# Sliding-window attention and an MLP on one core: more blocks' q and k transposed by DMA, and v's loads asked for first

## The chip, the cores and the metric

The kernel runs on one core of a Trainium2 chip. The metric is the device time of one execution in microseconds. The kernel before took a median of 314.43 us over three runs (312.98, 314.43 and 316.19). The profiled execution is a fourth one and took 316.07 us.

## The reference

Eight batches of eight heads attend over 576 tokens with 64 elements per head, in a causal window of 128 tokens with a linear distance bias per head. The result, laid out as 512 elements per token, is normalised without a bias, goes through an MLP with a hidden width of 2048, and is added to the MLP's output.

```python
scores = scale * np.matmul(q, k.transpose(0, 1, 3, 2))
mask = (rel >= 0) & (rel < window)                    # window = 128
scores = np.where(mask, scores + bias[None], -1000000000.0)
attn = np.exp(scores - np.max(scores, axis=-1, keepdims=True))
attn = attn / (np.sum(attn, axis=-1, keepdims=True) + 1e-09)
x = np.matmul(attn, v)                                # then (B, S, H * D)
xn = (x - mu) / np.sqrt(var + 1e-06) * g_ln
out = x + np.maximum(xn @ w_ch1, 0.0) @ w_ch2
```

## The kernel before

**Blocks and groups.** Two batches form a pair and a pair has nine blocks of 128 tokens, 36 blocks in all, numbered 0 to 35 in the list `order`. Within a pair, blocks 0 to 7 alternate between the two batches, and the ninth (`T = 8`) holds the last 64 tokens of both. An even block of a pair brings q and k for itself and its odd neighbour. So in the running numbers, q and k arrive with blocks 0, 2, 4, 6, 8, then 9, 11, 13, 15, 17, then 18, 20, 22, 24, 26, then 27 and so on; 8, 17, 26 and 35 are the tails. The MLP takes the blocks in groups: four groups of two blocks, then seven groups of four. Group 4 is blocks 8 to 11, group 5 is blocks 12 to 15.

**Loads.** The list `loads` (L247 to L256) holds, block by block, q and k (where the block is even in its pair) and then v, with the weights in between. `load_until` (L259) issues this list up to a place; the step of block n asks for everything up to block `n + AHEAD`, with one more block for n above 8 (L675). All these loads convert from float32 to float16 and are issued by POOL. The engines PE, DVE, ACT and SP run in the order in which the program emits their instructions. POOL is left to the compiler's own planner, which issues what it finds ready.

**Turning q and k.** The scores need q and k with the head's elements on the partitions. There are two ways. Up to block 17, `load_qk` (L198) loads two neighbouring tokens in one piece, so that a packet writes 256 bytes, with two DMAs for q and two for k. Then `turn` (L300) transposes 64x64 pieces on PE through `transposed` (L284): 64 transposes for a block (32 for a tail). DVE and ACT copy the result out of PSUM, with two copies each (one each for a tail). From block `TURN_BY_DMA = 18` on, `load_natural` (L211) loads single tokens (128 bytes a packet), with four DMAs for q and two for k. Then `turn_natural` (L321) issues DMA transposes on SP's queue: two for q and two for k (one each for a tail).

**Buffers.** The loaded q and k stand in `raw_pool`, four buffers each. A load waits until the block four earlier in the list of q and k has been turned. The turned q and k stand in `turned_pool`, four buffers each. v stands in ten buffers, so a load of v for block n waits for the last reader of block n - 10, which is `values_at_once` of block n - 8.

**The steps.** A hand-written list of steps is woven between the MLP's matmuls by `weave_at`. For n from 8 on, block n gives four steps (L674 to L692): the loads, the masks, `values_at_once` of n and `centre` of n with half of the scores of block n + 2; then the other half, with `turn` of block n + 3 where it is turned on PE; then masks, the square of n, and `turn_natural` of q for block n + 4 and of k for block n + 5 where these are turned by DMA; then masks again. `centre` (L512) makes `xc` on DVE and, from block 8 on, issues one DMA transpose on SP that writes the block's columns of the group's `xT`. `mlp1` of a group reads all of `xT`. SP also issues the output stores.

**The gain g.** `g_line` (one partition) and `g_row` (128 partitions) are constants, used by `spread_g`, by a copy in `turn_first`, and by `centre` of blocks 0 to 3 (L531). The output tiles `o` come from `out_pool`, with five buffers under one tag.

Of the kernel before, what the change touches and what calls it, by code (L numbers as in the profile page):

```python
# [10 lines left out]
FP16 = mybir.dt.float16  # L11
FP32 = mybir.dt.float32
# [5 lines left out]
P = 128  # L18
# [6 lines left out]
HALF = P // 2  # L25
GROUPS = [2] * 4 + [4] * 7

NV = 10
AHEAD = 6

FIRST_GROUPS, FIRST = 2, 4

# [3 lines left out]

SEVEN = 4

TURN_BY_DMA = 18


SUMS_AT = {
# [30 lines left out]
def kernel(  # L73
# [12 lines left out]
    DM = H * D  # L86
# [3 lines left out]
    HP = H // 2  # L90
# [4 lines left out]
    def pool(name, bufs, **kw):  # L95
        return ctx.enter_context(tc.tile_pool(name=name, bufs=bufs, **kw))

    consts = pool("consts", 1)
    raw_pool = pool("raw", 4)
    turned_pool = pool("turned", 4)  # L100
    probs_pool = pool("probs", 4)
    x_pool = pool("x", 14)
    xc_pool = pool("xc", 5)
# [2 lines left out]
    out_pool = pool("outp", 5)  # L106
# [30 lines left out]

    g_sb = consts.tile([P, NKB], FP32)
    nc.sync.dma_start(out=g_sb, in_=moe_g_ln.rearrange("(kb p) -> p kb", p=P))
    g_line = consts.tile([1, DM], FP32)  # L140
    nc.sync.dma_start(out=g_line, in_=moe_g_ln.rearrange("(o d) -> o d", o=1))
    g_row = consts.tile([P, DM], FP32)
    one_line = consts.tile([1, P], FP32)
    magic = consts.tile([P, 4], I32)
    ones = consts.tile([P, 4 * P], FP16)
# [87 lines left out]
    def by_dma(p, blk):  # L233
        return p * NSLOT + blk >= TURN_BY_DMA

# [9 lines left out]
    order = [(p, blk) for p in range(NPAIR) for blk in range(NSLOT)]  # L245
    w1s, w2s = ([(f, c) for c in range(4)] for f in (load_w1, load_w2))
    weights = {3: w1s + w2s[:2], 5: w2s[2:]}  # L247
    loads, place = [], []
    for n, (p, blk) in enumerate(order):
        if blk % 2 == 0:  # L250
            for src, tag in ((q, "q"), (k, "k")):
                load = load_natural if by_dma(p, blk) else load_qk
                loads.append((load, src, tag, p, blk // 2))
        loads.append((load_v, p, blk))
        place.append(len(loads))
        loads += weights.get(n, [])  # L256
    issued = 0
# [11 lines left out]
    turned = {}  # L269
# [30 lines left out]
    def turn(p, i, in_sc=False, copies=(nc.vector.tensor_copy, nc.scalar.copy)):  # L300

        ps = [bank(b if in_sc else None) for b in range(2)]
        k = keys_tile("k", p, i)
        if i < 4:
            q = queries(p, i)
            transposed("q", p, i, [t[:, 0] for t in ps])  # L310
            transposed("k", p, i, [t[:, 1] for t in ps])
            for b, copy in enumerate(copies):
                copy(out=q[:, b], in_=ps[b][:, 0])
                copy(out=k[:, b].rearrange("p h (c r) -> p r h c", r=2), in_=ps[b][:, 1])  # L314
        else:
            q = keys_tile("q", p, i)
            for tag, t, dst, copy in zip("qk", ps, (q, k), copies):
                transposed(tag, p, i, [t[:, 0]])
                copy(out=dst[:, 0].rearrange("p h (c r) -> p r h c", r=2), in_=t[:, 0])

    def turn_natural(tag, p, i):  # L321

        st = raw.pop((tag, p, i))
        t = turned_pool.tile([P, HP, 2, P], FP16, tag=tag, name=tag)
        turned[tag, p, i] = t.rearrange("p h b q -> p b h q")
        for b in range(2 if i < 4 else 1):
            nc.sync.dma_start_transpose(
                out=t[:, :, b], in_=st[:, b].rearrange("p h d -> p (h d)")
            )
# [6 lines left out]
        )  # L336

    def queries(p, i):
        t = turned_pool.tile([P, 2, 2, HP, HALF], FP16, tag="q", name="q")
        turned["q", p, i] = t.rearrange("p b r h c -> p b h r c")  # L340
        return t

    def keys_tile(tag, p, i):
        t = turned_pool.tile([P, 2, HP, P], FP16, tag=tag, name=tag)
        turned[tag, p, i] = t
        return t

    def turn_first():

        q, k = queries(0, 0), keys_tile("k", 0, 0)  # L350
        ps = [bank(b)[:, 0] for b in range(2)]
        transposed("q", 0, 0, ps)
        for b in range(2):
            nc.vector.tensor_copy(out=q[:, b], in_=ps[b])
        ps_row = spread_g()
        warm(2)
        ps = [bank(b)[:, 0] for b in (0, None)]
        transposed("k", 0, 0, ps)
        for b, copy in enumerate((nc.scalar.copy, nc.vector.tensor_copy)):
            copy(out=k[:, b].rearrange("p h (c r) -> p r h c", r=2), in_=ps[b])  # L360
        nc.vector.tensor_copy(out=g_row, in_=ps_row)
# [67 lines left out]
    def attends(p, blk):  # L429

        low, high, every = [0, 1], [2, 3], [0, 1, 2, 3]
        if blk == T:
            return [(p, T, [6, 7], m_ends, "probs", hps) for hps in (low, high)]
        if blk < 2:
            return [(p, blk, [blk], m_full[:, :, P:], "own", every)]
        return [(p, blk, [blk - 2, blk], m_full, "probs", hps) for hps in (low, high)]
# [5 lines left out]
    def tail_attend(p):  # L442
        return (p, T, [T], m_tail, "own", [0, 1, 2, 3])
# [166 lines left out]
    for g, size in enumerate(GROUPS):  # L610
        n = sum(GROUPS[:g])
# [3 lines left out]
    count = len(order)  # L615

    def turn_step(n, *how):
        p, blk = order[n]
        return [(turn, p, blk // 2) + how]

    def scores_step(n):
        return [(scores,) + order[n]]

    def values_steps(n):
        p, blk = order[n]
        ahead = place[min(n + AHEAD + (n > TURN_BY_DMA - 10), count - 1)]
        return [
            [(load_until, ahead), (masks, p, blk), (values, p, blk, 0)],
            [(values, p, blk, 1), (centre, p, blk)],
        ]  # L630

    def x_step(n, copy=nc.vector.tensor_copy):
        return [(turn_x,) + home[n] + order[n] + (copy,)] if n < BY_DMA else []

    def variance_of(n):

        return [(variance, n)] + [(inv_std, n - 3, 4)] * (n % 4 == 3)

    def masks_of(n, *halves):
        return [(masks,) + order[n] + halves]  # L640

    def warm_step(n):
        return [[(warm, n)]]


    steps = warm_step(11) + [[(turn_first,)]] + warm_step(3)
    steps += [scores_step(0), scores_step(1) + masks_of(0) + masks_of(1)] + warm_step(6)
    steps += values_steps(0)
    steps += [turn_step(2, True, (nc.scalar.copy, nc.scalar.copy))]
    steps += values_steps(1) + warm_step(4)  # L650
    steps += [x_step(0, nc.scalar.copy)] + warm_step(2) + [scores_step(2)]
    steps += [masks_of(2, 1) + x_step(1) + scores_step(3), values_steps(2)[0]]
    steps += [masks_of(2)]
    first = len(steps)
# [10 lines left out]
    steps += [values_steps(5)[0], turn_step(6, True), values_steps(5)[1], scores_step(6)]  # L665
    steps += [x_step(5) + masks_of(6), scores_step(7) + variance_of(4), values_steps(6)[0]]

    steps += [values_steps(6)[1], x_step(6) + masks_of(7), *values_steps(7)]
    steps += [x_step(7) + variance_of(5) + variance_of(6)]
    steps += [turn_step(8) + variance_of(7), scores_step(8) + turn_step(9)]  # L670
    steps += [[(scores_tail, 0)] + scores_step(9) + masks_of(8)]


    for n in range(8, count):  # L674
        ahead = place[min(n + AHEAD + (n > TURN_BY_DMA - 10), count - 1)]  # L675
        todo = []
        if n + 1 < count and order[n + 1][1] == T:
            todo.append(tail_attend(order[n][0]))
        if n + 2 < count:
            todo += attends(*order[n + 2])  # L680
        step = [(load_until, ahead), (masks,) + order[n]]
        step += [(values_at_once,) + order[n], (centre,) + order[n]]
        step += [(attend, *args, 1) for args in todo[:1]]
        second = [(attend, *args, 1) for args in todo[1:]]
        if n + 3 < count and order[n + 3][1] % 2 == 0 and not by_dma(*order[n + 3]):
            second += turn_step(n + 3)
        third = [(masks, *args[:2], 1) for args in todo[:1]] + [(square, n)]
        for tag, m in (("q", n + 4), ("k", n + 5)):
            if m < count and order[m][1] % 2 == 0 and by_dma(*order[m]):
                p, blk = order[m]  # L690
                third.append((turn_natural, tag, p, blk // 2))
        steps += [step, second, third, [(masks, *args[:2], 1) for args in todo[1:]]]  # L692
# [355 lines left out]
```

## Time and profile before

| | us |
|---|---|
| Median of three runs (lowest, highest) | 314.43 (312.98, 316.19) |
| The profiled execution | 316.07 |
| Its span, first to last instruction | 314.3 |
| Mean granted TensorE clock over the span | 0.994 |
| DVE busy, ACT busy, POOL busy | 233.9, 184.4, 107.9 |
| 64x64 transposes of q and k on PE (L294) | 576, of which 320 after 58 us |
| DMA transposes on SP: xT, k, q | 28, 18, 18 |
| Their time from issue to landing, median: xT, k, q | 4.4, 4.2, 5.5 |

A group of instructions has a line of the kernel, an engine, the tiles that it writes and reads, a count, its busy time and the mean of one. Idle time ahead of an instruction is put down to whatever released it last. The chain of waits follows the last instruction back to what it waited for; in its listing each row has a start, a length and a name. PE's instructions overlap, so the busy time of PE doesn't say how fast it works; the granted clock beside it does.

### The profile page before, as it was taken

What the parts mean: (1) busy time and instruction counts of PE and PEld (TensorE: products, weight loads), DVE (VectorE), ACT (ScalarE), POOL (GpSimd) and SP (SyncE); (2) the same over time, 40 slices, a digit from 0 to 9 for tenths busy, and PEclk for the clock granted to TensorE, in tenths of its full rate; (3) what the DMA queues carried; (4) which work ended last, traced back from release to release, by engine and by line L of the source; (5) the groups of instructions that cost most, each with busy time, mean ns of one, the idle gap of its engine ahead of it and who ended that gap; (6) DMA issues with size and microseconds to landing.
All of it is one profiled execution on the core that took longest, in us unless ns stands there. A gap on an engine that the chain in (4) does not pass through costs nothing.

```text
span 314.3 us, 9387 instructions
## 1 busy us (share of the span) xinstructions
PE 302.9 (96%) x3886; PEld 200.8 (64%) x3886; DVE 233.9 (74%) x629; ACT 184.4 (59%) x330; POOL 107.9 (34%) x148
## 2 busy tenths in 40 slices
PE   8889999998988999999999999999999999999994
PEld 3468655856733568755864686468656865785583
DVE  2689887697993889767976887688769876964563
ACT  6588766767944983467357735753676268405600
POOL 8923758769341634725251645120000000000000
PEclk9999999999997999999999999999999999999999
DMA  9999999999992999999999999993562143025004
GB/s 105 176 206 198 189 146 173 199 146 151 131 117 53 95 105 125 138 197 106 134 126 166 101 141 138 165 135 59 114 108 50 37 94 79 17 19 134 0 19 117
DMA packets 140316, 36.99 MB, mean 118 GB/s; under 512 B 131185, under 2 KB 135921, under 8 KB 140274
## 3 DMA queue, kind: packets, MB, share of 16 engines
q0 software_dynamic: 98560, 18.36, 85.2%
q1 hardware_dynamic: 41234, 17.52, 32.9%
q8 instruction: 30, 0.49, 0.7%
q10 hardware_dynamic: 480, 0.52, 0.5%
q14 instruction: 12, 0.10, 0.1%
HBM read 36.90 MB, written 9.44 MB: 147 GB/s over the span
## 4 chain that ended last, share of the span: by engine, by line
PE 83%; DVE 6%; DMA 5%; ACT 2%; POOL 2%; issue 1%; POOLq 0%
PE ps_m L718 39%; PE ps_s L810 24%; PE ps_sc L407 5%; PE ps_m L748 5%; PE ps_q L889 4%; PE ps_sc L489 4%; DMA k<-in_k_dram 2%; DMA xT<-xc 2%; DMA out_dram<-o 1%; ACT probs L415 1%; PE ps_pv L460 1%; POOL q L204 1%; DVE w L768 1%; DVE k L314 1%; DVE st L565 1%
## 5 line engine op out<-in xcount | busy, mean ns | idle before, releaser
L718 PE MATMUL ps_m<-xT,w1g 128*128 128x512 f16 (+1 forms) x576 | 119.5, 359 | 2.7 <-DMA xT<-xc 2.4
L734 ACT ACTIVATE ht_all<-ps_m 128x512 f16<-128x512 f32 (+1 forms) x159 | 81.9, 519 | 42.8 <-PE ps_m L718 40.6
L718 PEld LDWEIGHTS <-w1g 128*128 128x128 f16 x576 | 54.3, 98 | 54.1 <-issue 5.9
L415 ACT ACTIVATE probs<-ps_sc 128x1024 f16<-128x1024 f32 x56 | 56.6, 1029 | 48.0 <-PE ps_sc L407 48.0
L239 POOL DMA_DIRECT2D vx<-in_v_dram x40 | 34.5, 867 | 33.4 <-PE ps_sc L489 24.8
L810 PE MATMUL ps_s<-w,s 128*128 128x256 f16 x384 | 43.8, 273 | 0.0
L810 PEld LDWEIGHTS <-s 128*128 128x128 f16 x384 | 36.7, 98 | 4.7
L426 DVE TENSOR_TENSOR probs<-probs,m 128x1024 f16<-128x1024 f16 x56 | 36.9, 683 | 1.7 <-ACT probs L415 1.7
L810 PE MATMUL ps_s<-w,ht_all 128*128 128x256 f16 x288 | 34.3, 273 | 0.0
L768 DVE TENSOR_TENSOR s<-ht_all 128x1024 f16<-128x1024 f16 (+2 forms) x35 | 20.4, 582 | 18.3 <-ACT ht_all L734 17.7
L228 POOL DMA_DIRECT2D q<-in_q_dram x32 | 21.9, 703 | 30.2 <-DMA q<-q 23.5
L748 PE MATMUL ps_m<-w,ht_all 128*128 128x512 f16 x128 | 31.0, 380 | 0.0
L810 PEld LDWEIGHTS <-ht_all 128*128 128x128 f16 x288 | 27.4, 98 | 5.0
L831 DVE SCALAR_TENSOR_TENSOR o<-ps_s,rstd,x 128x256 f32<-128x256 f32 x48 | 21.0, 479 | 11.1 <-PE ps_s L810 11.1
L407 PE MATMUL ps_sc<-q,k 64*64 64x128 f16 (+1 forms) x1088 | 24.0, 209 | 0.9 <-ACT probs L415 0.8
L407 PEld LDWEIGHTS <-k 64*64 64x64 f16 x1088 | 15.9, 106 | 12.8 <-issue 10.3
L571 ACT ACTIVATE junk<-xc 128x512 f16<-128x512 f16 x28 | 17.6, 627 | 4.9 <-DVE xc L540 4.8
L498 DVE SCALAR_TENSOR_TENSOR x<-ps_sc,rec 128x512 f16<-128x512 f32 x28 | 19.4, 692 | 1.0
L831 DVE SCALAR_TENSOR_TENSOR o<-ps_s,rstd,o 128x256 f32<-128x256 f32 x36 | 15.7, 479 | 4.5 <-PE ps_s L810 4.4
L748 PEld LDWEIGHTS <-ht_all 128*128 128x128 f16 x128 | 11.2, 98 | 11.2
L225 POOL DMA_DIRECT2D k<-in_k_dram x16 | 14.4, 916 | 10.9 <-DMA k<-k 10.9
L415 ACT ACTIVATE own<-ps_sc 128x1024 f16<-128x1024 f32 x12 | 12.1, 1032 | 9.2 <-PE ps_sc L407 9.2
(88 smaller groups left out, 343.4 us busy)
## 6 DMA issues: line engine op xcount, KB each, us to landing
out_dram<-o SPq DMA_DIRECT2D x66, 128.0 KB, 3.5
k<-in_k_dram POOLq DMA_DIRECT2D x32, 128.0 KB, 6.0
vx<-in_v_dram POOLq DMA_DIRECT2D x32, 128.0 KB, 6.6
w<-in_moe_w_ch_dram POOLq DMA_DIRECT2D x8, 512.0 KB, 10.5
q<-in_q_dram POOLq DMA_DIRECT2D x40, 64.0 KB, 4.2
q<-in_q_dram POOLq DMA_DIRECT2D x16, 128.0 KB, 7.2
k<-in_k_dram POOLq DMA_DIRECT2D x8, 64.0 KB, 4.8
vx<-in_v_dram POOLq DMA_DIRECT2D x8, 64.0 KB, 4.7
```

The costliest lines, as they stand in the source:

```text
L228: nc.gpsimd.dma_start(out=t[half, b], in_=tokens.rearrange("h (c r) d -> r c h d", r=2)[r],)
L239: nc.gpsimd.dma_start(out=vx[p0 : p0 + n, :, 0:D], in_=v[b, :, t0 : t0 + n, :].rearrange("h p d -> p h d"),)
L407: nc.tensor.matmul(in_halves(ps[cols, j, n, t, :])[:, r, queries], kt[rows, hp, cols], in_halves(qt[rows, b, hp])[:, r, queries], start=Tr ...
L415: nc.scalar.activation(out=dst.rearrange("p (n j) q -> p j n q", j=2), in_=ps.rearrange("p j n t q -> p j n (t q)"), func=AF.Exp, scale=in ...
L426: nc.vector.tensor_tensor(out=dst, in0=dst, in1=mask, op=ALU.mult)
L498: nc.vector.scalar_tensor_tensor(out=x.rearrange("p (h d) -> p h d", h=H), in0=ps[:, :, 0:D], scalar=1.0, in1=rec.unsqueeze(2).broadcast_t ...
L718: nc.tensor.matmul(ps[:, 0:cols], w[:, kb, fb * P : (fb + 1) * P], xT[:, kb, 0:cols], start=(kb == 0), stop=(kb == NKB - 1),)
L734: nc.scalar.activation(out=ht[:, fb, :], in_=ps[:, 0:cols], func=AF.Relu)
L748: nc.tensor.matmul(sums[at], ht[:, fb, at * P : (at + 1) * P], w2[:, fb, :], start=(fb == 0), stop=(fb == NFB - 1),)
L768: nc.vector.tensor_tensor(out=out, in0=a, in1=b, op=op)
L810: nc.tensor.matmul(ps[:, pair, :], lhs[:, fb, at : at + P], rhs[:, fb, :], start=(first and pair == 0 and fb == 0), stop=(fb == half - 1), ...
L831: nc.vector.scalar_tensor_tensor(out=outs[at][:, cols], in0=ps[:, pair], scalar=rstd[:, n : n + 1], in1=(xs[p, blk] if fresh else outs[at] ...
```

## The change

- `TURN_BY_DMA` is 13 in place of 18: blocks 13, 15 and 17 are loaded by `load_natural` and turned by `turn_natural`.
- `turn_natural` stands one block sooner in the steps: q of block n + 5 and k of block n + 6. Since k of block 13 would then belong to block 7's steps, it is written out there by hand.
- The turned q keep four buffers, the turned k get five.
- `g_line` and `g_row` are no constants any more but take two of the rotating output tiles.
- `AHEAD` is 7 for all blocks; before it was 6 for blocks up to 8 and 7 after.
- From block 20 on, v's load stands ahead of q's and k's in the list of loads.

```diff
-AHEAD = 6
+AHEAD = 7
...
-TURN_BY_DMA = 18
+TURN_BY_DMA = 13
+V_FIRST = 20
...
-    turned_pool = pool("turned", 4)
+    turned_pool = {"q": pool("turned_q", 4), "k": pool("turned_k", 5)}
...
-    g_line = consts.tile([1, DM], FP32)
+    g_line = out_pool.tile([P, DM], FP32, tag="o", name="g_line")[0:1]
...
-    g_row = consts.tile([P, DM], FP32)
+    g_row = out_pool.tile([P, DM], FP32, tag="o", name="g_row")
...
     for n, (p, blk) in enumerate(order):
+        of_v = [(load_v, p, blk)]
+        if n >= V_FIRST:
+            loads += of_v
         if blk % 2 == 0:
             for src, tag in ((q, "q"), (k, "k")):
                 load = load_natural if by_dma(p, blk) else load_qk
                 loads.append((load, src, tag, p, blk // 2))
-        loads.append((load_v, p, blk))
+        if n < V_FIRST:
+            loads += of_v
...
-        ahead = place[min(n + AHEAD + (n > TURN_BY_DMA - 10), count - 1)]
+        ahead = place[min(n + AHEAD, count - 1)]
...
+    first_by_dma = order[TURN_BY_DMA][0], order[TURN_BY_DMA][1] // 2
...
-    steps += [x_step(7) + variance_of(5) + variance_of(6)]
+    steps += [x_step(7) + variance_of(5) + variance_of(6) + [(turn_natural, "k") + first_by_dma]]
...
-        for tag, m in (("q", n + 4), ("k", n + 5)):
+        for tag, m in (("q", n + 5), ("k", n + 6)):
             if m < count and order[m][1] % 2 == 0 and by_dma(*order[m]):
```

More of the change, by code (lines that the diff above doesn't have):

```diff
@@ L323, in turn_natural @@
         st = raw.pop((tag, p, i))
-        t = turned_pool.tile([P, HP, 2, P], FP16, tag=tag, name=tag)
+        t = turned_pool[tag].tile([P, HP, 2, P], FP16, tag=tag, name=tag)
         turned[tag, p, i] = t.rearrange("p h b q -> p b h q")
@@ L338, in queries @@
     def queries(p, i):
-        t = turned_pool.tile([P, 2, 2, HP, HALF], FP16, tag="q", name="q")
+        t = turned_pool["q"].tile([P, 2, 2, HP, HALF], FP16, tag="q", name="q")
         turned["q", p, i] = t.rearrange("p b r h c -> p b h r c")
@@ L343, in keys_tile @@
     def keys_tile(tag, p, i):
-        t = turned_pool.tile([P, 2, HP, P], FP16, tag=tag, name=tag)
+        t = turned_pool[tag].tile([P, 2, HP, P], FP16, tag=tag, name=tag)
         turned[tag, p, i] = t
@@ L674 @@
     for n in range(8, count):
-        ahead = place[min(n + AHEAD + (n > TURN_BY_DMA - 10), count - 1)]
+        ahead = place[min(n + AHEAD, count - 1)]
         todo = []
```

## The prediction, made before the change was run

> **What bounds the kernel now.** First the page's busy times, then what PE waited for:
>
> ```profile
> PE 302.9 (96%) x3886; PEld 200.8 (64%) x3886; DVE 233.9 (74%) x629; ACT 184.4 (59%) x330; POOL 107.9 (34%) x148
> ```
>
> ```profile
> PE ps_m L718 <- DMA xT<-xc: 2.4, 1, 2.4
> PE ps_warm L276 <- DVE vx L991: 1.5, 1, 1.5
> PE ps_sc L407 <- ACT probs L415: 0.8, 3, 0.5
> ```
>
> PE is busy for 302.9 of 314.3 us and sets the end. Its longest wait is a single one of 2.4 us for a DMA transpose of `xT`; no other wait on the list is charged to a transpose or a load of v. Third, the chain of waits in order of time, around that wait:
>
> ```profile
> 84.32 0.60 DVE w L768
> 84.92 0.34 DVE q L313
> 85.26 0.64 DVE k L314
> ...
> 89.44 5.77 DMA xT<-xc
> 95.21 0.25 issue
> 95.45 4.44 PE ps_m L718 x12
> ...
> 102.80 0.56 PE ps_tr L294 x63
> ...
> 114.38 0.57 PE ps_tr L294 x31
> ```
>
> Up to 89 us DVE sets the pace, and two of its rows are the copies of block 13's turned q and k. Then `xT` of block 11, the last block of group 4, takes 5.77 us to land, and `mlp1` of group 4 starts at 95.45. From there on PE sets the pace, and the turns of blocks 15 and 17 stand on the chain. Fourth, the stretches around the wait (columns: stretch, length, busy time and count of PE, PEld, DVE, ACT and POOL, clock, DMA share, GB/s):
>
> ```profile
> 85.00:90.00 5.00, 5.00 (x67) 2.59 (x65) 4.89 (x12) 3.87 (x7) 5.00 (x7) 1.00 1.62 90
> 90.00:95.00 5.00, 3.04 (x15) 1.18 (x12) 4.79 (x14) 0.74 (x3) 0.16 (x1) 1.00 1.89 150
> 95.00:100.00 5.00, 4.55 (x21) 1.90 (x22) 0.42 (x3) 1.27 (x3) 0.00 (x0) 0.66 0.23 55
> ```
>
> After the wait the clock is 0.66 over five microseconds; cut finer, it is 0.50 from 95.7 to 99.1. So 12 matmuls took 4.44 us, where 20 on a full clock take 4.32 (the chain's row at 131.50): 12 x 0.216 = 2.59, so the slow clock cost 4.44 - 2.59 = 1.85 us more. The wait is worth 2.4 + 1.85 = 4.3 us in all.
>
> **The change, part by part.** The sum is made against the profiled execution (316.07 us: the span of 314.3 and 1.77 around it), which lies 1.64 above the median of 314.43; I carry differences over to the median.
>
> *Turns taken from PE.* Blocks 15 and 17: the chain's rows of 0.56 and 0.57, both where nothing but PE sets the pace, so 1.13 us is gained. Block 13: PE's transposes at 83.98 to about 84.6 take 0.6 us, but the wait for `xT` follows; they only bring PE sooner to it, at 93.03 - 0.6 = 92.4. They are worth nothing unless `xT` is sooner too.
>
> *Copies taken from DVE and ACT.* Block 13's on DVE are 0.34 + 0.64, and the queue behind them moves up by 1.0 us: masks, then the values' division and `xc` of block 11. Nothing else holds these: `values_at_once` of block 11 is on PE at 86.40, which with 0.6 gone ends at about 86.45, when DVE would be ready for it at 87.6 - 1.0 = 86.6. So `xT` of block 11 is issued at 88.4, not 89.44. ACT's copies (0.59 + 0.76 for block 13, the same for 15, 0.73 for 17) lie beside PE; ACT's idle time before its score activations is 48.0 us in all, so I take nothing.
>
> *New DMA transposes on SP.* Ten: k of 13 (two) in block 7's steps, q of 13 (two) behind `xT` of block 8, k of 15 (two) behind `xT` of 9, q of 15 (two) behind `xT` of 10, then k and q of 17 (one each) behind `xT` of 11 and 12. Eight of them go ahead of `xT` of block 11. SP takes about 1.2 us for one (L327's medians are 1.22 for k and 1.21 for q). `xT` of block 10 is issued at 84.35, so SP is through at 84.35 + 3 x 1.2 = 88.0, just before 88.4: SP itself costs nothing, with 0.4 us to spare. If a transpose waited for its load, everything behind it on SP would wait: stores and `xT`. The loads of 13 and 15 landed at 64 to 73 us before; 4 us later still leaves those of 15 five or more ahead of 81. k of 13 may hold SP until some 70 us, where a store of group 2 at 69.31 gives way for 2 or 3 us; `xT` of block 8 follows at 73.84, so this is hidden, and a longer hold would cost only once it reached 88 us.
>
> *What the transposes do to the landing.* This is the open cost. With loads in flight, `xT` lands 5.77 us after issue; with none, at 102.00, it landed after 2.8. Two transposes of q issued at 117.2 and 118.5, among loads and close behind an `xT`, took 6.1 and 6.0. The longest of L327's took 7.0. `xT` of block 11 will have two of q right ahead of it and loads beside it, so the bounds are 2.8 and 7.0. I take 6.1: it is nearest to the row at 117.2. Then 88.4 + 6.1 + 0.25 (the chain's issue row) = 94.75, against 95.45: 0.7 sooner. PE idles 2.35 us, as long as now, so the slow clock stays.
>
> *Loads.* Blocks 13 and 15 go from four DMAs of 0.68 us on POOL (L204) to four of 0.70 (L228) and two of 0.92 (L225): +1.9 each; 17 from 0.58 to 0.71 four times: +0.5. That is 4.4 us, and POOL idled 4.8 us at 80 to 84.8, waiting for PE's turn of 13; this cover is used up. Their packets halve to 128 bytes and double to 10,240. Without cover it delays loads that are used 25 us later or more (k of 18, loaded at 77, is transposed at 109.7), so it costs nothing by itself, only through the landing above: the loads of block 20, at 84.8 to 90 now, will still run beside `xT` of 11.
>
> The Trainium skill (DMA: Bandwidth & Descriptors, "Issuing engines are not separate DMA queues") says that DMAs from all engines run on the same 16 DMA engines and interleave, which speaks against a landing of 2.8 us here and agrees with 5.77 beside loads.
>
> *The rest.* Turning one block sooner moves pairs of transposes past one `xT` each on SP, from block 18 on. One pair stood between two `xT` already, so the queue is as long; group 6 has its last `xT` issued at 153.16 and needed at 162.16, group 7 at 184.04 and 193.29. PE waits for nothing there, so nothing can be gained, and without those 9 us an `xT` would cost as group 4's does. `AHEAD`, the fifth buffer and g's tiles: g_row is last read by the `xc` at 25.9 us, the fourth output tile is written at 54.7, so no one waits; with more early outputs a store would. v first: v of 20 must wait for the values of 12 anyway (POOL idled 10.49 us for it up to 100.66). Zero.
>
> Sum: 1.13 + 0.7 = 1.8 us off: 314.2 for the profiled execution, **312.6** against the median.
>
> **The rivals.**
>
> *The wait goes.* If loads of 20 come sooner, because the buffer of 13 is free after a DMA at about 82 in place of PE at 84.7, or later, because v of 20 now stands ahead of them on POOL, then `xT` of 11 lands as at 102.00: 88.4 + 2.8 + 0.25 = 91.45, before PE's 92.4. Gain: 95.45 - 92.4 + 1.85 + 1.13 = 6.0, so 310.1. Halfway, idle 1.2 us on a full clock: 311.3. For: the list of loads. Against: POOL doesn't follow the list (it issued v of 19 between two DMAs for k of 20), and DMA was busy from 56 to 84 without the new packets.
>
> By the Trainium skill (TensorE: Matmul & The Clock Gate, "Why this matters for your kernels") it takes idle gaps over some 3 us to throttle PE; here 2.4 us did, so the measurement decides. By the rule the slow clock wouldn't be there to gain, and this case would end at 310.1 + 1.85 = 312.0.
>
> *The queue is late (slower).* The place is `xT` of 11 behind q of 15 on SP. Some transposes hold SP for up to 2.6 us; two of these would move the issue to 84.35 + 1.2 + 5.2 = 90.75, and with 7.0 to land PE starts at 98.0. That is 2.55 later, less 1.13, plus another slow stretch of 1.7: 317.5. It decides once PE starts over 1.13 us later than now, after 96.6.
>
> The skill's section "Why small descriptors are slow (HBM only)" of the DMA page gives every packet a fixed cost; the doubled packets point this way.
>
> *The landing eats what DVE gave.* `xT` is issued at 88.4 and lands at 95.2 to 96.3: 313.3 to 314.4. Also the case in which v first and the sooner turns don't do what they say, since PE never waited there.
>
> **How the numbers follow.** Forecast 0.45 (311.3 to 313.5 with the spread of the runs), the wait goes 0.28 (309.8 to 311.8), eaten 0.15, late 0.12. One per cent, about what a measurement of this kernel tells from no change, is 3.1 us: 311.3 and 317.6. Faster: most of the second case and the low edge of the first, 0.33. Slower: those of the late case that reach 317.6 or beyond, and what I can't see, 0.10. Same: 0.57. The range takes all but the ends of the second and the fourth: 309.8 to 316.3.
>
> **What would show it.** PE's start on group 4 at about 94.8 with a wait of some 2.3 us for `xT`, landing about 6 us after an issue at 88.4; no L294 after 75 us; SP rows of L327 from 68 us; clock 0.5 for one stretch after the wait. It is wrong if PE waits in a new place (scores of 13 or 15 for q or k, or `xT` of a later group), or if `xT` of 11 is issued later than 89.

## The result: the changed kernel is slower, and its profile

The changed kernel takes a median of 318.63 us (317.50 to 319.48, six runs), the kernel before 313.77 us beside it (312.98 to 316.19, six runs). The ratio is 1.0137 (95% interval 1.0101 to 1.0174): 1.4% slower. The forecast was 312.6 us in a range of 309.8 to 316.3, so the forecast change had the wrong sign, and the time lies outside the range.

The profiled execution of the changed kernel took 317.5 us (span 315.4, mean granted clock 0.986). It is the quickest of its six, while that of the kernel before (316.07) is among its slowest. So the two traces differ by 1.4 us and the medians by 4.9; the section on the prediction comes back to this.

The line of busy times in the changed kernel's page:

```profile
PE 300.7 (95%) x3726; PEld 198.8 (63%) x3726; DVE 232.5 (74%) x624; ACT 181.7 (58%) x325; POOL 112.1 (36%) x152
```

PE has 160 instructions fewer (3726 for 3886) and 2.2 us less to do, yet the span is 1.1 us longer. What PE waited for longest, from the list of waits (total, times, longest):

```profile
PE ps_m L727 <- DMA xT<-xc: 5.3, 1, 5.3
PE ps_warm L284 <- DVE vx L1000: 1.5, 1, 1.5
PE ps_sc L415 <- ACT probs L423: 1.0, 4, 0.5
```

It is the old wait, now 5.3 us in place of 2.4; there is no new one. The chain in order of time (start, length, what):

```profile
86.22 1.41 PE ps_m L757 x6
...
87.92 0.14 PE ps_m L757
88.05 9.13 DMA xT<-xc
97.19 0.05 issue
97.23 4.84 PE ps_m L727 x12
```

`xT` of block 11 is issued at 88.05, 1.4 us sooner than before. DVE has no copies of block 13 to make and is through with `xc` at 87.61, by its timeline:

```profile
87.26 0.35 DVE L548 TENSOR_SCALAR xc<-x,mean 128x512 f16<-128x512 f16 x1
```

But the `xT` takes 9.13 us to land, where it took 5.77. The stretches around it (columns as in the prediction):

```profile
85.00:90.00 5.00, 5.00 (x67) 2.59 (x65) 4.61 (x11) 2.98 (x6) 3.46 (x5) 1.00 1.84 130
90.00:95.00 5.00, 1.92 (x9) 0.69 (x7) 3.80 (x13) 0.00 (x0) 0.89 (x1) 0.97 1.70 151
95.00:100.00 5.00, 2.77 (x7) 1.01 (x8) 0.00 (x0) 0.60 (x1) 3.60 (x5) 0.50 2.01 191
100.00:105.00 5.00, 5.00 (x63) 2.41 (x62) 1.91 (x6) 3.00 (x5) 4.29 (x7) 0.85 2.34 160
```

Before, the DMA share fell to 0.23 in 95 to 100; now it stays at 1.7 or more throughout. And the clock is 0.50 for 6.83 us (94.66 to 101.48) in place of 3.4. What stands on SP's queue ahead of that `xT`, from SP's timeline (start, time on SP, line, operation, count):

```profile
76.05 2.62 SPq L335 DMA_TRANSPOSE q<-q  x2
78.82 1.25 SPq L558 DMA_TRANSPOSE xT<-xc  x1
80.24 3.24 SPq L335 DMA_TRANSPOSE k<-k  x2
83.81 1.26 SPq L558 DMA_TRANSPOSE xT<-xc  x1
85.24 2.73 SPq L335 DMA_TRANSPOSE q<-q  x2
88.05 2.97 SPq L558 DMA_TRANSPOSE xT<-xc  x1
```

SP takes on nine transposes in 12 us. In the trace they land in the order of issue: the second q of block 13 at 85.17, then `xT` of block 9 at 86.61, k of 15 at 87.54 and 91.06, `xT` of 10 at 92.34, q of 15 at 94.08 and 95.84, and `xT` of 11 at 97.19. Seven transposes land in the 12.0 us after 85.17, one in 1.7 us. Their packets, 512 for each, begin one transpose after another with hardly a gap, those of `xT` of block 9 from 84.07 to 85.59 and those of `xT` of block 11 from 94.35 to 95.78. SP puts transposes in faster than they come out, so each new `xT` lands later after its issue: 5.4 us for block 8, then 7.8, 8.5 and 9.1.

From the restart to the end of the span the changed kernel needs 218.15 us and the one before 218.84. These 0.7 us fit the turns of 15 and 17 (1.13 gained) less the longer slow clock (4.84 for the 12 matmuls, before 4.44).

### The profile page after: what moved, and what is told of

It is laid out like the page before. It is cut to its first block, busy times and chain, and to the rows that moved or that the text cites. A ratio compares the mean times of both kernels' runs of the same rounds, so it can differ in the third digit from the quotient of the medians.

```text
span 315.4 us, 9090 instructions
## 1 busy us (share of the span) xinstructions
PE 300.7 (95%) x3726; PEld 198.8 (63%) x3726; DVE 232.5 (74%) x624; ACT 181.7 (58%) x325; POOL 112.1 (36%) x152
## 4 chain that ended last, share of the span: by engine, by line
PE 88%; DMA 5%; ACT 2%; POOL 2%; DVE 2%; issue 1%; POOLq 0%
PE ps_m L727 40%; PE ps_s L819 24%; PE ps_m L757 8%; PE ps_sc L415 6%; PE ps_sc L497 4%; PE ps_q L898 4%; DMA xT<-xc 3%; DMA k<-in_k_dram 2%; ACT probs L423 1%; PE ps_pv L468 1%; POOL q L208 1%; POOL k L208 1%; PE ps_sc L302 1%; POOL vx L243 1%; PE ps_tx L568 0%
## 5 line engine op out<-in xcount | busy, mean ns | idle before, releaser
L777 DVE TENSOR_TENSOR s<-ht_all 128x1024 f16<-128x1024 f16 (+2 forms) x35 | 20.4, 583 | 18.7 <-ACT ht_all L743 18.1
L232 POOL DMA_DIRECT2D q<-in_q_dram x40 | 27.5, 705 | 14.4 <-DMA q<-q 12.2
L229 POOL DMA_DIRECT2D k<-in_k_dram x20 | 17.6, 888 | 27.5 <-DMA k<-k 23.8
```

What stands on the lines that cost most here:

```text
L232: nc.gpsimd.dma_start(out=t[half, b], in_=tokens.rearrange("h (c r) d -> r c h d", r=2)[r],)
L777: nc.vector.tensor_tensor(out=out, in0=a, in1=b, op=op)
```

## Experiments

The first theory: `xT` of block 11 lands late because block 15's four transposes stand ahead of it on SP. Its rivals: the loads (POOL waited 5.43 us for block 13's k buffer, which the planner gave to block 15, so loads may be pushed into the stretch), v first and the sooner steps, and the transposes by themselves, with no part for the loads. Each ratio is to the kernel before on the same chip (314.05 us beside the first four kernels, 314.23 beside the next four, 314.83 beside the last four).

**Block 15's transposes behind `xT` of block 11.**

```diff
-        for tag, m in (("q", n + 5), ("k", n + 6)):
+        for tag, m in (("q", n + 5), ("k", n + 6), ("q", n + 4), ("k", n + 4)):
+            if (m == 15) != (m == n + 4):
+                continue
```

> The changed kernel, with the four DMA transposes of block 15's k and q moved behind xT of block 11 (both in block 11's steps). POOL's order of loads stays as changed. If the four transposes queued ahead of xT of block 11 make it land late (9.1 us after issue in the changed kernel), it lands after some 6 us, PE waits 2 to 2.5 us for it in place of 5.3, and the time falls from 318.6 to 312 to 314.5. If the loads pushed back by POOL's wait of 5.4 us are the cause, the landing stays near 9 us and the time at 317 to 319. If neither, the wait is unchanged too.

315.94 us, ratio 1.0039 (1.0002 to 1.0076). From its chain:

```profile
88.03 6.98 DMA xT<-xc
95.01 0.14 issue
```

Issued at the same moment as in the changed kernel, the same `xT` lands 2.2 us sooner, and PE waits 2.8 us. With block 15's transposes behind it, more than half of the loss is gone, though less than was expected. The landing, 7 us, is still above 5.77; a packet of instructions that took 1.83 us at 88.6 lies in it. And `xT` of block 10 took 8.27 us in this run (84.19 to 92.47), with no other transpose ahead of it once `xT` of block 9 had landed at 87.43. From 86 to 88 us no packet of a transpose began, while some 1,200 packets of loads began per microsecond. So a transpose can be late without a line ahead of it.

**k of block 13 later, so that block 15's load takes another buffer.** `turn_natural` of k for block 13 is emitted with the turn of block 8.

```diff
-    steps += [x_step(7) + variance_of(5) + variance_of(6) + [(turn_natural, "k") + first_by_dma]]
-    steps += [turn_step(8) + variance_of(7), scores_step(8) + turn_step(9)]
+    steps += [x_step(7) + variance_of(5) + variance_of(6)]
+    steps += [turn_step(8) + variance_of(7) + [(turn_natural, "k") + first_by_dma], scores_step(8) + turn_step(9)]
```

> The changed kernel, with block 13's k turned one step later in the program (behind the turn of block 8), so that the load of block 15's k takes the buffer of block 8 and not that of block 13, and POOL should not wait at 66 to 72 us. The transposes ahead of xT of block 11 stay. If the pushed-back loads are the cause: the wait for xT falls to 2 to 3 us and the time to 312 to 315. If the transposes alone are the cause: the wait stays near 5 us and the time at 317 to 319. If both share it: 315 to 317.

319.54 us, ratio 1.0178 (1.0143 to 1.0214): no better. POOL's wait is gone (none of over 2 us between 55 and 94), and PE's is 6.1 us. POOL's wait is not the cause. SP's timeline shows how the numbers are shared out here:

```profile
82.11 3.55 SPq L335 DMA_TRANSPOSE k<-k  x2
85.75 1.29 SPq L558 DMA_TRANSPOSE xT<-xc  x1
87.21 4.87 SPq L335 DMA_TRANSPOSE q<-q  x2
92.18 1.39 SPq L558 DMA_TRANSPOSE xT<-xc  x1
```

Block 15's q hold SP for 4.87 us, so `xT` of block 11 is issued at 92.18 and not at 88; it then lands after 7.48 us. The hold was longer and the landing shorter, and the end is as late as before.

**All of the change but the turns of blocks 13, 15 and 17**, which stay on PE (v first, sooner steps, `AHEAD`, five buffers and g's tiles stay as changed):

```diff
-TURN_BY_DMA = 13
+TURN_BY_DMA = 18
...
-    steps += [x_step(7) + variance_of(5) + variance_of(6) + [(turn_natural, "k") + first_by_dma]]
+    steps += [x_step(7) + variance_of(5) + variance_of(6)]
```

> The changed kernel with blocks 13, 15 and 17 turned on PE again (DMA turns from block 18 on); all else of the change stays: one block sooner, five buffers, g's tiles, v first, seven blocks ahead. If the turns of 13, 15 and 17 by DMA are the cause, by transposes or by loads, this is the kernel before again: 313 to 315 with a wait for xT of up to 2.4 us. If turning sooner or v first costs, it stays above 316.

314.85 us, ratio 1.0025 (1.0008 to 1.0041). These edits cost 0.8 us (0.3 to 1.3) of the 4.9. Its chain serves below:

```profile
90.04 5.43 DMA xT<-xc
95.47 0.24 issue
95.71 2.75 PE ps_m L727 x12
```

PE waited 2.07 us here, and the 12 matmuls took 2.75 us: the clock stayed full.

**Four more transposes in the kernel before**, where block 15's would stand, into tiles that nobody reads (g's rows move to output tiles to make room):

```diff
+    def dummy(tag, p, i):
+        flat = raw[tag, p, i].rearrange("p h r d -> p (h r d)")
+        for b in range(2):
+            nc.sync.dma_start_transpose(
+                out=scratch[tag][:, :, b], in_=flat[:, b * DM : (b + 1) * DM]
+            )
...
+        if n == 9:
+            third.append((dummy, "k", 1, 3))
+        if n == 10:
+            third.append((dummy, "q", 1, 3))
```

> The kernel before, plus four extra DMA transposes on SP at the places where the changed kernel turns block 15: two of its loaded k behind xT of block 9 and two of its loaded q behind xT of block 10, into tiles that nothing reads (g's rows lie in output tiles to make room). Loads, PE and the copies stay as before. If transposes ahead of xT of block 11 are enough to make it late, its landing goes from 5.8 to 8 or 9 us and the time from 313.8 to 317 or more. If the pushed-back loads are needed for it, the landing stays at 6 to 7 us and the time within 1 us of 314.5.

316.48 us, ratio 1.0071 (1.0043 to 1.0099): about half of the loss. PE's timeline around the wait:

```profile
91.70 1.46 PE L764 MATMUL ps_m<-w,ht_all 128*128 128x512 f16 x6
95.87 1.44 PE L734 MATMUL ps_m<-xT,w1g 128*128 128x512 f16 x3 [2.71 <-DMA out_dram<-o]
```

The profile names a store as what ended the wait, as this store uses the semaphore of an earlier `xT`; `xT` of 11 landed at 95.74. It is issued at 89.56 and lands after 6.18 us, not 9.13, which looked as if the transposes were not enough. The order of landing says otherwise: `xT` of block 9 landed at 85.37, the six transposes behind it up to 95.74, one in 1.73 us, the same pace as in the changed kernel. What the changed kernel has on top is block 13's transposes ahead of `xT` of block 9 (landed at 86.61, 1.24 later), and PE, which has no turn of 13, comes to the wait 1.3 us sooner (91.9 for 93.2). Together these two, 2.5 us, are the difference between a wait of 2.7 and one of 5.3 us.

**What the late `xT` costs: blocks 10 and 11 of `xT` turned on PE** and copied by ACT, all else as changed.

```diff
+X_ON_PE = (10, 11)
...
-        if n >= BY_DMA:
+        if n >= BY_DMA and n not in X_ON_PE:
...
+        if n in X_ON_PE:
+            third.append((turn_x,) + home[n] + order[n] + (nc.scalar.copy,))
```

> The changed kernel, with xc of blocks 10 and 11 transposed on PE and copied by ACT, not by DMA; all the rest of the change stays, the four transposes of block 15 and the late loads too. If the whole loss is the late landing of group 4's last xT, with the slow clock after it, PE's wait of 5.3 us and the slow clock go and the time falls from 318.6 to 310 to 312.5, under the kernel before. If the change costs elsewhere as well (scores waiting for q or k, later groups), it stays above 314.

311.78 us, ratio 0.9921 (0.9888 to 0.9954). Its stretches:

```profile
85.00:90.00 5.00, 5.00 (x75) 2.73 (x70) 4.64 (x11) 3.62 (x7) 4.88 (x7) 1.00 1.95 172
90.00:95.00 5.00, 5.00 (x28) 2.41 (x27) 4.28 (x8) 2.18 (x5) 1.68 (x3) 1.00 2.28 139
95.00:100.00 5.00, 5.00 (x67) 2.62 (x66) 4.02 (x15) 3.99 (x7) 3.26 (x5) 1.00 2.53 179
```

PE is busy throughout and the clock is full, with the DMA engines as loaded as in the changed kernel. So the loss came through group 4's `xT`: without that wait the kernel is below the one before, with the 0.8 us of the other edits still in it.

**Packets of 256 bytes for blocks 13 and 15**: loaded in pairs of tokens as before, and turned by DMA from that layout (the scores are of other pairs of tokens).

```diff
-                load = load_natural if by_dma(p, blk) else load_qk
+                load = load_natural if p * NSLOT + blk >= 17 else load_qk
...
+            half = st[:, b] if p > 1 or i == 4 else st.rearrange("p (b h) r d -> p b h (r d)", b=2)[:, b]
...
-                out=t[:, :, b], in_=st[:, b].rearrange("p h d -> p (h d)")
+                out=t[:, :, b], in_=half.rearrange("p h d -> p (h d)")
```

> The changed kernel, with q and k of blocks 13 and 15 loaded in pairs of tokens as before (256 bytes a packet, half as many packets) and still transposed by DMA, straight from that layout. So the tokens and heads of these two blocks stand in another order than the scores assume, and their scores are of other pairs; all sizes, counts and places are kept. If the doubled packets of the loads fill the DMA engines beside xT of block 11, the landing falls from 9.1 to some 7 us and the time to 315 to 317. If the packets' size doesn't matter, it stays at 318 to 319.

319.81 us, ratio 1.0150 (1.0098 to 1.0201), a wait of 6.1 us. The smaller packets of these two blocks are not the cause.

**Another place for PE's instruction packet.** In the changed kernel's trace a packet of 16 KB of instructions at 88.3 coincides with the start of this `xT`, and from 88 to 90 us half as many packets of loads and transposes began (943) as in the two microseconds before (1,811). 46 tiny matmuls in place of 6 warming ones at the start move it.

```diff
-    steps = warm_step(11) + [[(turn_first,)]] + warm_step(3)
+    steps = [[(pad, 46)]] + warm_step(5) + [[(turn_first,)]] + warm_step(3)
```

> The changed kernel, with 46 tiny matmuls on PE at its start in place of six of the eleven warming ones, so that PE's stream has 40 matmuls with their weight loads more ahead of everything. In the changed kernel a packet of 16 KB of instructions (queue 8) goes through at 88.3 us, and all packets around it take 1 us longer, just as xT of block 11 is transposed; in the kernel before it goes at 85.5, ahead of that. With 80 more rows ahead it should go at about 85.5 again. If the instruction packet makes up 1 to 1.5 us of the landing, the landing falls from 9.1 to 7.5 or 8 us and the time by 1 to 2 us, to 316.5 to 317.5. If not, nothing moves by more than 0.5 us.

319.47 us, ratio 1.0137 (1.0089 to 1.0185). The packet came at 89.7, later and not sooner, block 15's q held SP for 4.44 us, and PE waited 5.1. The run doesn't say what the packet costs. (The expectation has all packets around it 1 us longer. In the changed kernel's trace single packets that began just behind it took up to 1.2 us; the mean of those that began from 88 to 89 us is 0.05 to 0.06.)

**By DMA from block 15 on, block 15's behind `xT` of 11** (block 13 stays on PE; the edit of the first experiment, with `TURN_BY_DMA = 15` and no k of 13 in block 7's steps).

> The changed kernel with DMA turns from block 15 on (13 on PE again), and block 15's four DMA transposes in block 11's steps, behind xT of block 11. No new transpose stands ahead of that xT, and POOL has no wait for block 13's k. What is left of the change there is 1.9 + 0.5 us more loading for blocks 15 and 17. If transposes and pushed-back loads are what made xT late, the landing is 5.5 to 6.5 us, PE waits 2 to 3 us, and 1.1 us of PE is saved: 312.5 to 314.5. If the doubled packets of block 15 and 17's loads do it, the landing is 7 us or more and the time over 315.

313.47 us, ratio 0.9953 (0.9912 to 0.9995). With nothing but `xT` and stores on SP from 70 to 90 us, the last `xT` is issued at 90.18 and lands after 5.6; PE waits 2.2 us on a full clock.

By then the theory had changed: SP's queue is one line that drains at some 1.7 us a transpose beside loads. What the loads do to that pace was open; the first experiment, in which the last two `xT` took 5.0 and 2.5 us behind the one ahead, shows that it is not fixed.

**Fewer loads beside it**: the changed kernel without the load of block 20's q (its scores are made from block 18's q).

```diff
     def load_natural(src, tag, p, i):
+        if (tag, p, i) == ("q", 2, 1):
+            raw[tag, p, i] = raw[tag, 2, 0]
+            return
```

> The changed kernel without the load of block 20's q (its scores are made from block 18's q, which stays in its buffer). That takes four DMAs and 2,048 packets of 128 bytes out of the stretch from 85.8 to some 95 us, beside the xT of block 11; the four transposes of block 15 stay ahead of it on SP. If the landing comes of loads and transposes sharing the DMA engines, xT of block 11 (issued at 88.05, landing 9.13 in the changed kernel) lands within 7.5 us, PE starts group 4 before 95.8, and the median is 315 to 316.5. If the four transposes ahead in SP's queue set it alone, it still takes over 8.5 us and the median stays at 317.5 or more.

318.30 us, ratio 1.0103 (1.0063 to 1.0144). POOL's timeline shows why this decides nothing about loads:

```profile
84.93 2.06 POOL L235 DMA_DIRECT2D q<-in_q_dram  x3
87.69 0.68 POOL L235 DMA_DIRECT2D q<-in_q_dram  x1 [0.70 <-DMA k<-in_k_dram]
```

The planner put the next block's four q DMAs into the free place, so the stretch held as many loads as ever (6,883 packets from 85 to 97 us, in the changed kernel 6,111). What is left is one more execution of the same line of transposes, and SP's timeline and the chain show it with the numbers shared out otherwise:

```profile
86.06 4.60 SPq L338 DMA_TRANSPOSE q<-q  x2
90.75 1.27 SPq L561 DMA_TRANSPOSE xT<-xc  x1
```

```profile
90.75 7.12 DMA xT<-xc
97.87 0.05 issue
97.91 4.99 PE ps_m L730 x12
```

SP was held, the issue came 2.7 us later than in the changed kernel, the landing was 2.0 shorter, and PE started 0.7 later. Over the five kernels with this line of transposes, from the landing of block 13's second q to that of `xT` of block 11:

| | `xT` of 11 issued | to landing | PE starts | seven transposes land in |
|---|---|---|---|---|
| changed kernel | 88.05 | 9.1 | 97.23 | 12.0 |
| k of 13 later | 92.18 | 7.5 | 99.70 | 11.9 |
| pairs | 91.03 | 7.7 | 98.80 | 12.0 |
| instruction packet moved | 92.27 | 7.2 | 99.50 | 12.9 |
| without block 20's q | 90.75 | 7.1 | 97.91 | 12.5 |

Issue and landing vary by 4.2 and 2.0 us; the time in which the line drains, by one. (In the two rows without a landing of their own, pairs and the moved packet, PE's start stands for it.)

**Block 11 of `xT` on PE in the kernel before** (`X_ON_PE = (11,)`, the edit as above): what the wait was worth there.

> The kernel before, with only the columns of block 11 in xT transposed on PE and copied by ACT, so that group 4's last xT isn't a DMA. It measures what the wait is worth in the kernel before. By the prediction's price (2.4 us of wait and 1.85 of slow clock, less some 0.4 for four transposes on PE) the median falls by 3.9, to about 310.2. If the slow clock doesn't follow the wait in most executions, only 2.0 is gained: 312.1. If the transposes wait for DVE's xc and PE is held anyway, nothing: 314.

312.25 us, ratio 0.9914 (0.9880 to 0.9948), with no wait and a full clock. It gains 2.6 us, not the 3.9 that the prediction's price of the wait would give.

**Block 11 alone on PE in the changed kernel.**

> The changed kernel with block 11 alone turned on PE; block 10's xT stays on SP, issued at 83.81 with a landing of 8.53 in the changed kernel, so it is there at 92.3, when PE comes at about 91.9 + 0.3. If only the last xT is late, the median is that of the kernel with blocks 10 and 11 turned on PE less a PE turn: 311.0 to 312.0. If what is late is SP's queue as a whole, PE now waits for xT of block 10 for a microsecond or more and it is 313 to 315.

312.25 us, ratio 0.9911 (0.9876 to 0.9945). From its waits:

```profile
PE ps_m L733 <- DMA xT<-xc: 1.1, 1, 1.1
```

PE now waits for `xT` of block 10, which was issued at 85.38 and landed 9.16 us later, with block 13's and k of 15 ahead of it. So the line as a whole is late, and not only its last member, but a wait of 1.1 us costs little and leaves the clock full.

**By DMA from block 15 on, and block 11's `xT` on PE** (block 15's transposes behind the place of `xT` of 11, as in the first experiment).

> The kernel in which blocks from 15 on are turned by DMA, with block 15's transposes behind the xT of block 11 (313.47 in its run, a wait of 2.24 us for that xT), and now block 11's xT turned on PE. If that wait is all that is left there, it falls by 2.24 less 0.3, to about 311.5, no better than the changed kernel with its two blocks on PE (311.78 in its run). If the PE turn of block 13 was hidden by the wait, another 0.6 comes back: 312.1.

311.46 us, ratio 0.9892 (0.9852 to 0.9932), the lowest median of all. PE and its clock in 40 slices, from its page:

```profile
PE   8889999999999999999999999999999999999994
...
PEclk9979999999999999999999999999999999999999
```

The hole at 90 to 100 us is gone. (The 7 in the clock is a slow stretch from 18.7 to 22.1 us, far from this wait.) Beside the kernel before with the same edit (312.25) that is 0.8 us for taking blocks 15 and 17 from PE, but the intervals overlap, so this gain is not settled.

## Why the prediction was wrong

**The step that failed is the landing**: "I take 6.1", with bounds of 2.8 and 7.0. It was 9.13 us. I used the landing as a delay that each transpose has by itself. It is a line: seven transposes land in 12 us while SP issues them within 10.6, and the last one pays for all ahead of it; from 83.8 to 88.1 every issue made it five on their way. The trace of before showed a line, too, behind the very row of 7.0 that I took as the upper bound: a q issued at 137.5 landed at 144.5, and the three transposes behind it at 145.3, 145.5 and 145.9. POOL had issued its last load there at some 139, and the line ran off fast once those loads were through. From 76 to 97 us packets of loads begin in every microsecond, and no row of before shows so long a line under loads from end to end; the 7.0 was no bound for it.

**The second step that failed follows from it**: PE "idles 2.35 us, as long as now, so the slow clock stays". With 5.3 us of idle time a second slow stretch followed, and all six executions of the changed kernel have a mean clock of 0.980 to 0.989. In the trace the second one cost 0.4 us only (4.84 for 4.44), since the clock fell at 94.66, before PE started again.

**"SP itself costs nothing, with 0.4 us to spare"** was wrong as well, though the issue came near the forecast (88.05, predicted 88.4). SP was through with q of 15 at 87.97, as reckoned. But `xc` was ready at 87.61, 1.8 us sooner than before and not 1.0, so `xT` waited 0.4 us for SP. Two misses cancelled, so the nearness is luck. In four experiments block 15's q held SP for up to 4.9 us and the issue came at 90.75 to 92.27. It made little difference, since the line drained no faster.

**The price of the wait was taken from an execution that is not typical.** I carried differences from the profiled execution (316.07, clock 0.994) over to the median. Of 49 executions of the kernel before whose clock is known (a fiftieth, of 318.64 us, is left out), 36 have a mean clock of 0.997 or more, and their median is 314.02 us; the other 13 have a median of 316.09. A stretch of 3.4 us at 0.50 alone would bring the mean to 0.995. So most executions have no slow stretch after the wait, and there was no 1.85 us to gain in the median. The run with block 11 on PE agrees: 2.6 us gained in place of 3.9. The 1.85 was a little too much, too: on a full clock the 12 matmuls took 2.75 us where they were measured (the run with the turns of 13, 15 and 17 on PE), not 2.59, so the slow stretch cost 4.44 - 2.75 = 1.7. The untypical execution also explains most of the difference between profiles and medians. Between the two traces the loss is 1.78 (later start) - 0.7 = 1.1 us of span; against a typical execution of before, the changed kernel pays the 1.7 of a first slow stretch as well, near 3 us, and the profiled execution was the quickest of its six by 1.0. What made the other five slower, at much the same clock, isn't shown.

**Right were** PE's arrival at the wait (91.92, predicted 92.4), the turns of 15 and 17 as 1.13 us on the path of the trace (the restart to the end is shorter by that less the clock's share), and that no other wait appears. In the medians the 1.13 us don't show: with no wait, the changed kernel with two blocks of `xT` on PE (0.9921) is not measurably faster than the kernel before with one (0.9914). "The rest", which I put at zero, cost 0.8 us (0.3 to 1.3), in places that weren't looked for. That the loads of blocks 13 and 15 cost "nothing by itself" holds as far as the size of their packets goes (the run with pairs). The loads' share in the landing was the part that I left without a price.

**The rival that came true in its outcome** is "the queue is late", with a chance of 0.12: its place (`xT` of 11 behind q of 15 on SP), the point from which it decides (a start after 96.6; it was 97.23) and another slow stretch. It reckoned with a hold of SP and 7.0 us of landing, for a start at 98.0, and with 1.7 us for the slow stretch, for 317.5 us. In the trace there was no such hold, the landing was longer and the slow stretch cost 0.4; where SP was held, the landing was shorter. Hold and landing are two sides of one thing, the line that doesn't drain.

In the rival "The wait goes" the times (310.1 and 311.3) are counted from the profiled execution, where the forecast and the other rivals are counted from the median. In the forecast's way they would be 308.4 and 309.6, below the range. As the wait grew, nothing hangs on it here.

The Trainium skill (DMA: Bandwidth & Descriptors, "Queues, rings and completion order") says that SP's DMAs have one ring on each DMA engine and that an engine takes packets from the rings in turn. The traces fit that as far as what the line gets depends on the loads; that transposes land in the order of issue is what these traces show, not the section. Between 90 and 96 us of the changed kernel 337 packets of transposes and 497 of loads began per microsecond; a transpose has 512, so one takes 1.5 us. From 144 to 145 us of the kernel before 727 and 6 began, and from 115 to 116 of the changed one 1,006 and 80, which is 0.5 to 0.7 us for one. From 86 to 88 us of the first experiment no packet of a transpose began beside the loads, though `xT` of block 10 had been issued at 84.19; why isn't shown. The prediction used another section of that page, on interleaving, for a single landing, and didn't ask how long the line was.

So loads slow the line two- or threefold. That is read from these stretches; the run that was to show it in the place itself kept its loads. What an instruction packet in the midst of the line costs stays open. In the microsecond behind the one at 88.3 us hardly anything moved (8 GB/s from 89 to 90 us, 151 and 141 in the microseconds beside it), so it may well be one of the line's 12.0 us, but no run takes it out.

## What to carry to other kernels

Before moving work to a DMA queue, count what will be in flight there at once (the rate of issue times the time to landing); if loads run beside it all the time, the single landings of a trace are no bounds, and the pace at which the queue drains beside loads has to be estimated in their place. A transfer that PE waits for should not stand behind others that are needed 10 us later: turning one block of `xT` on PE, or issuing block 15's transposes behind it, was worth far more than the transposes taken from PE. And look whether the profiled execution is a typical one, by its time and its clock, before carrying a price from it to the median.

## What the runs showed of the hardware that was not expected

SP is not always through with a DMA transpose in 1.2 us: with several on their way, one held it for 2 to 3.5 us (3.25 in the run without block 20's q, 3.51 in the changed kernel with block 11 alone on PE).

An idle PE lost its clock by steps. Waits of 1.1, 2.07 and 2.24 us left it full, one of 2.42 us (the kernel before, profiled), 2.71 and 2.84 brought 3.4 us at 0.50, and 5.1 to 6.1 brought 6.8 us. The Trainium skill (TensorE: Matmul & The Clock Gate, "Why this matters for your kernels") warns of gaps over some 3 us; here the step lay between 2.24 and 2.42 us, and the kernel before, close to it, took it in 14 of 50 executions at most. (At most, as a lowered mean has other causes too: the profile with DMA turns from block 15 on has its one slow stretch at 15.5 to 18.9 us.)

Packets of 16 KB of instructions (queue q8 in the page's third section, 29 of them in the changed kernel) took about 1 us each. That they are PE's is inferred: 29 x 16 KB is 64 bytes for each of PE's 7,452 matmuls and weight loads. In the changed kernel, with transposes and loads beside them, packets of 128 and 256 bytes that began just behind one took up to 1.6 us, where their mean is near 0.04 us.
